# An attention-and-maxout kernel: stores moved between half-size DMA transposes, loads one batch earlier, a warmed-up head

## The chip, the cores and the metric

The kernel runs on one core of a Trainium2 chip. A core has five engines that run their own instruction streams and wait for each other through semaphores: TensorE (PE, matrix products), VectorE (DVE), ScalarE (ACT), GpSimd (POOL) and SyncE (SP), which only issues transfers. Sixteen DMA engines move data between the main memory (HBM), and the on-chip memory (SBUF), and inside SBUF. Matrix products land in PSUM, eight banks of 128 x 512 float32, and VectorE or ScalarE must copy them out ("evict") before a bank can be used again.

A transfer is started by an engine's instruction stream. GpSimd builds its descriptors in software ("software queue" below), SyncE in hardware ("hardware queue"). A stream is in order: an instruction that waits holds up all that stand behind it on that engine, transfers included.

The metric is device time in microseconds, the median of several runs.

## The reference

Four batches of 12544 rows of 128 numbers. First an induced-set attention: 32 learned points attend to all rows (`h`), then all rows attend to these 32 results. Then a maxout layer on each row.

```python
h = mab(I, x)                 # softmax(I x^T / sqrt(128)) x : 32 x 128 for each batch
y = mab(x, h)                 # softmax(x h^T / sqrt(128)) h : 12544 x 128 for each batch
# maxout on all 50176 rows, d_ff = 1024
h1 = y @ w1
h2 = y @ w2
g = np.maximum(h1, h2)
out = g @ w_out
```

Since `y = a h / sum(a)`, with `a` the 32 exponentials of a row, and the sum is positive, the kernel never forms `y`. It uses max(h1, h2) = h1 + relu(h2 - h1), so

    out = (a (h w1 w_out) + relu(a (h (w2 - w1))) w_out) / sum(a)

The first term needs only a 32 x 128 matrix for each batch (called m1 in the code, from w1*w_out); the second needs a product of depth 32, a relu of 1024 numbers for each row, and a product of depth 1024.

## The kernel before

A batch is 98 chunks of 128 rows. Phase 1 of a batch (the sums that give h) must be complete before its second part can begin; so phase 1 of batch b+1 is put between the work of batch b. The program is ordered by hand: a small model of the engines' times in the Python code (`ck`) decides in which order the instructions are issued; the chip sees only that order and the waits.

Loads convert float32 to float16 on the way, in 14-chunk parts (7 for each batch), into 12 buffers `xn`. The scores need x transposed (`xT`, two tiles, one for even and one for odd batches). In batch 0 TensorE transposes; for batches 1 to 3 a DMA transpose does.

```python
    outp = ctx.enter_context(tc.tile_pool(name="outp", bufs=5))     # output tiles, 128 x 512 f32
    ...
    def load_x(b, i):
        k0, n = parts[b][i]
        nc.gpsimd.dma_start(out=xn_at[b, i][:, 0:n, :], in_=xr[b, :, k0 : k0 + n, :])

    def transpose_x_dma(b, i):
        k0, n = parts[b][i]
        nc.sync.dma_start_transpose(xT_tiles[b % 2][:, k0 : k0 + n, :], xn_at[b, i][:, 0:n, :])
```

The head. TensorE transposes batch 0 (`p1_transpose`, L216; VectorE copies the first half of each part out of PSUM, L220, ScalarE the second, L223), makes the scores (L232), ScalarE takes the exponential (L241), and two accumulations in PSUM sum up (L253, L262). Then the weights:

```python
        n0 = len(parts[0])                      # 8 parts in batch 0
        for i in range(n0):
            p1_transpose(0, i)
            if i > 0:
                p1_accum(0, i - 1)
            p1_scores(0, i)
        p1_accum(0, n0 - 1)
        for i in range(7):
            load_x(1, i)
        small_h(0)                              # h of batch 0
        weights_1()                             # w2 - w1
        small_hwd(0)                            # hwd = h (w2 - w1), L336
        ...
        for i in range(7):
            transpose_x_dma(1, i)
        stage(blocks[0])                        # exponentials a of a block of rows, L449 and L461
        weights_2()                             # w1 transposed, L376; copies on ScalarE, L369 and L380
        weights_3()                             # w1*w_out, L387
        small_m1(0)                             # m1 = h w1 w_out, L350; m1bd, L357
        nstage = 1
```

The main loop. A block is four quarters of rows (four groups of 32 rows of the TensorE array work at once). `phase` (L718) makes four relu inputs of 128 x 512, in four PSUM banks; ScalarE (L734) or VectorE (L737), whichever the model has free earlier, evicts each with a relu: one such eviction is a "unit", worth four of the 128 x 128 products that follow. `final_one` (L562) multiplies with w_out, eight products for each chunk of 128 rows; a group of four chunks is then scaled by 1/sum(a) on VectorE into an output tile and stored:

```python
        def evict_group(g, end):
            osb = outp.tile([128, 4, C], F32, name=f"o_{uid[0]}", tag="o")
            nc.vector.tensor_mul(osb[...], g.ps[...], rp)                    # L588 and two more forms
            ...
            for b, c, s, m in runs:
                eng = nc.sync if b == B - 1 else nc.gpsimd
                eng.dma_start(out=outr[b, :, c : c + m, :], in_=osb[:, s : s + m, :])   # L614
            chunks_done[0] += n
```

The side work is called by the number of chunks done:

```python
        for b in range(1, B):
            base = DONE0[b - 1]                          # 0, 98, 196
            step, first = (5, 14) if b == 1 else (7, 4)
            for i in range(7):
                at(base + first + step * i, p1_scores, b, i)          # reads xT, part i
                at(base + first + step * i + 2, p1_accum, b, i)       # reads xn, part i
            end = base + first + step * 6
            at(end + 3, small_fold, b)                   # GpSimd: folds the sums of exponentials, L293, L294
            at(end + 5, small_h, b)                      # TensorE, L313: reads the fold
            at(end + 6, small_hwd, b)
            at(end + 7, small_m1, b)
            if b + 1 < B:
                for i in range(7):
                    at(base + 20 + 6 * i, load_x, b + 1, i)

        def staged_all(b):                               # when the last block of batch b is staged
            if 0 <= b and b + 2 < B:
                for i in range(7):
                    transpose_x_dma(b + 2, i)            # xT tile of batch b is free again
```

Between the accumulations, GpSimd adds up the exponentials of phase 1 (L283, L288). In this kernel all stores of batches 0 to 2 and all loads are GpSimd's; SyncE has the transposes and the stores of batch 3.

Of the kernel before, what the change touches and what calls it, by code (L numbers as in the profile page):

```python
# [9 lines left out]
F16 = mybir.dt.float16  # L10
# [98 lines left out]
def kernel(  # L109
# [15 lines left out]
    assert C == 128 and M == 32 and NJB == 8 and N % 128 == 0 and K == 98 and B == 4  # L125
    scale = 1.0 / math.sqrt(C)
    P1 = 14

    consts = ctx.enter_context(tc.tile_pool(name="consts", bufs=1))
    big = ctx.enter_context(tc.tile_pool(name="big", bufs=1))  # L130
# [1 line left out]
    e2p = ctx.enter_context(tc.tile_pool(name="e2p", bufs=4))  # L132
    smp = ctx.enter_context(tc.tile_pool(name="smp", bufs=2))
    relup = ctx.enter_context(tc.tile_pool(name="relup", bufs=2))
    outp = ctx.enter_context(tc.tile_pool(name="outp", bufs=5))
    rpp = ctx.enter_context(tc.tile_pool(name="rpp", bufs=4))
    psum = ctx.enter_context(tc.tile_pool(name="psum", bufs=1, space=bass.MemoryType.PSUM))

# [6 lines left out]
    def bank(shape, dtype=F32, only=None):  # L145
        i = min(range(8), key=lambda j: ck.bank[j]) if only is None else only
        uid[0] += 1
        return i, psum.tile(shape, dtype, name=f"ps{uid[0]}", tag=f"bank{i}", bufs=1)
# [14 lines left out]
        k0, n = parts[b][i]  # L163
        nc.gpsimd.dma_start(out=xn_at[b, i][:, 0:n, :], in_=xr[b, :, k0 : k0 + n, :])  # L164

    def transpose_x_dma(b, i):
        k0, n = parts[b][i]
        nc.sync.dma_start_transpose(xT_tiles[b % 2][:, k0 : k0 + n, :], xn_at[b, i][:, 0:n, :])

    identity16 = consts.tile([128, 128], F16, name="identity16")  # L170
    identity32 = consts.tile([128, 128], F32, name="identity32")
    ones32 = consts.tile([128, 128], F32, name="ones32")
    ones16 = consts.tile([128, 128], F16, name="ones16")
    ones_q = consts.tile([128, 4], F16, name="ones_q")

    ind_sb = consts.tile([M, C], F32, name="ind_sb")
# [11 lines left out]
    with tc.manual_schedule(engines={ET.PE, ET.DVE, ET.Activation, ET.Pool, ET.SP}):  # L188
# [7 lines left out]
        nc.gpsimd.dma_start(out=w2f, in_=moe_w2)  # L196
        nc.gpsimd.dma_start(out=w1f, in_=moe_w1)
        nc.gpsimd.dma_start(out=woutf, in_=moe_w_out.rearrange("(jb j) c -> j jb c", j=128))
        nc.vector.memset(ones16, 1.0)
        nc.vector.memset(ones32, 1.0)  # L200
        nc.vector.memset(ones_q, 0.0)
# [7 lines left out]
        def p1_transpose(b, i):  # L209
            k0, n = parts[b][i]  # L210
            xn = xn_at[b, i]
            h = (n + 1) // 2
            for g, m in ((0, h), (h, n - h)):
                bi, ps = bank([128, 8, 128], F16)
                for j in range(m):
                    nc.tensor.transpose(ps[:, j, :], xn[:, g + j, :], identity16)  # L216
                end = ck.run(0.056 * m, ready=ck.bank[bi], why="T")
                dst = xT_tiles[b % 2][:, k0 + g : k0 + g + m, :]
                if g == 0:
                    nc.vector.tensor_copy(out=dst, in_=ps[:, 0:m, :])  # L220
                    ck.bank[bi] = ck.on_dve(end, 0.08 + 0.075 * m)
                else:
                    nc.scalar.copy(out=dst, in_=ps[:, 0:m, :])  # L223
                    ck.bank[bi] = ck.on_act(end, 0.05 + 0.12 * m)
                st[b]["xT", i] = max(ck.bank[bi], st[b].get(("xT", i), 0.0))
# [170 lines left out]
            ck.bank[bi] = ck.on_dve(end, 0.2)  # L396


        bi, ps = bank([128, 512])
        nc.tensor.transpose(ps[:, 0:M], ind_sb, identity32[0:M, 0:M])  # L400
        nc.vector.tensor_copy(out=inducingT, in_=ps[:, 0:M])
        ck.bank[bi] = 0.0
        for n in ("h", "e"):
            st[0][n + "b"], st[0][n + "ps"] = bank([128, 512])
            ck.bank[st[0][n + "b"]] = INF
        n0 = len(parts[0])
        for i in range(n0):
            p1_transpose(0, i)
            if i > 0:
                p1_accum(0, i - 1)  # L410
            p1_scores(0, i)
        p1_accum(0, n0 - 1)
        for i in range(7):
            load_x(1, i)
        small_h(0)
        weights_1()
        small_hwd(0)


        blocks = []  # L420
        for b in range(B):
            c0 = 0
# [12 lines left out]
        def stage(blk):  # L435
            bi, ps = bank([128, 512])
            wd = blk.width
            some = [qu for qu in blk.quarters if qu]
            ck.wait(max(ck.bank[bi], st[some[0].b]["hT4r"]), "stage bank")
            for q in range(4):  # L440
                qu = blk.quarters[q] or some[0]
                hq = st[qu.b]["hT4"][:, 32 * q : 32 * (q + 1)]
                xT = xT_tiles[qu.b % 2]
                lo = qu.c0 if qu.c0 + wd <= K else K - wd
                pieces = [(0, qu.c0, min(wd, K - qu.c0))]
                if pieces[0][2] < wd:
                    pieces.append((pieces[0][2], lo, wd - pieces[0][2]))
                for t, c, n in pieces:
                    nc.tensor.matmul(  # L449
                        out=ps[32 * q : 32 * (q + 1), 128 * t : 128 * (t + n)],  # L450
                        lhsT=hq,
                        rhs=xT[:, c : c + n, :],
                        start=True,
                        stop=True,
                        tile_position=(0, 32 * q),
                        skip_group_check=True,
                    )
            end = ck.run(0.054 * wd, "col")
            uid[0] += 1
            blk.e2 = e2p.tile([128, 512], F16, name=f"e2_{uid[0]}", tag="e2")  # L460
            nc.scalar.activation(  # L461
                out=blk.e2[:, 0 : 128 * wd], in_=ps[:, 0 : 128 * wd], func=AF.Exp, scale=scale
            )
            blk.staged = ck.bank[bi] = ck.on_act(end, 0.05 + wd * 128 / 1200.0)
            blk.staged = max([blk.staged] + [st[qu.b]["hwdr"] for qu in some])
            blk.relu = {}

        relu_of = {}
# [1 line left out]
        def relu_slot(blk, q):  # L470

            if q in blk.relu:
                return blk.relu[q]
            w = blk.quarters[q].w
            tag = f"relu{q}" if w > 1 else f"rs{q}"
            past = relu_of.setdefault(tag, [])
            if len(past) >= 2 and past[-2].last_group[q] >= state["g"]:
                return None
            past.append(blk)
            uid[0] += 1  # L480
            blk.relu[q] = relup.tile([128, 1024 * (w if w == 1 else 4)], F16, name=f"relu_{uid[0]}", tag=tag)
            return blk.relu[q]

        def dens(blk):
            bi, ps = bank([128, 512])
            ck.wait(ck.bank[bi], "den bank")
            wd = blk.width
            for t in range(wd):
                nc.tensor.matmul(
                    out=ps[:, 4 * t : 4 * t + 4],  # L490
                    lhsT=blk.e2[:, 128 * t : 128 * (t + 1)],
                    rhs=ones_q,
                    start=True,
                    stop=True,
                )
            end = ck.run(0.029 * wd)
            uid[0] += 1
            blk.rp = rpp.tile([128, 4, 4], F32, name=f"rp_{uid[0]}", tag="rp")
            nc.vector.reciprocal(
                out=blk.rp[:, 0:wd, :].rearrange("p t q -> p (t q)"), in_=ps[:, 0 : 4 * wd]  # L500
            )
            ck.bank[bi] = ck.on_dve(end, 0.2)


        groups = [g for blk in blocks for g in blk.groups]
# [72 lines left out]
        def evict_group(g, end):  # L578
# [31 lines left out]
                else:  # L610
                    runs.append([qu.b, c, s, 1])
            for b, c, s, m in runs:
                eng = nc.sync if b == B - 1 else nc.gpsimd
                eng.dma_start(out=outr[b, :, c : c + m, :], in_=osb[:, s : s + m, :])  # L614
            chunks_done[0] += n

        def finals_left():
# [131 lines left out]

        for b in range(1, B):  # L750
            base = DONE0[b - 1]
            step, first = (5, 14) if b == 1 else (7, 4)
            for i in range(7):
                at(base + first + step * i, p1_scores, b, i)
                at(base + first + step * i + 2, p1_accum, b, i)
            end = base + first + step * 6
            at(end + 3, small_fold, b)
            at(end + 5, small_h, b)
            at(end + 6, small_hwd, b)
            at(end + 7, small_m1, b)  # L760
            if b + 1 < B:
                for i in range(7):
                    at(base + 20 + 6 * i, load_x, b + 1, i)

        def staged_all(b):
            if 0 <= b and b + 2 < B:
                for i in range(7):
                    transpose_x_dma(b + 2, i)

        pending = []  # L770

# [15 lines left out]
                pending.pop(0)  # L787
                f(*a)

        for i in range(7):  # L790
            transpose_x_dma(1, i)
        stage(blocks[0])
        weights_2()
        weights_3()
        small_m1(0)
        nstage = 1
        START = ck.pe
        while state["g"] < len(groups):
            side_work()
            need = [ptr[q][0] for q in range(4)]  # L800
            if nstage < len(blocks):
# [6 lines left out]
                if min(left) <= 3 and free and min(ck.bank) <= ck.pe + 0.1 and all(  # L808
                    "hT4" in st[qu.b] and "hwd" in st[qu.b] for qu in blocks[nstage].quarters if qu
                ):  # L810
                    stage(blocks[nstage])
                    nstage += 1
                    if nstage < len(blocks) and blocks[nstage].b != blocks[nstage - 1].b:
                        staged_all(blocks[nstage - 1].b)
                    continue
            jobs = plan_phase()
            tp = INF
# [48 lines left out]
```

## Time and profile before

| what | value |
|---|---|
| median of 3 runs | 386.44 us (375.67, 386.44, 393.12) |
| profiled run | 381.42 us, span of the core 379.6 us |
| TensorE busy | 344.5 us, 91% of the span |
| VectorE, ScalarE busy | 287.7 us (76%), 280.1 us (74%) |
| GpSimd busy | 84.2 us (22%) |
| DMA, software queue | 33.69 MB, 38.3% of 16 engines |
| DMA, hardware queue | 16.08 MB, 31.8% of 16 engines |
| transposes (21), us from issue to landing | median 9.3 |
| stores from GpSimd (72 of 256 KB), the same | median 4.5 |
| stores from SyncE (24 of 256 KB), the same | median 2.0 |

How to read it: "busy" of TensorE is modelled, since its products are pipelined, and is not a measure of how near it is to its peak. The profile's page cuts the span into 40 slices of 9.5 us; each digit is a tenth of the slice:

```profile
PE   2968999998979999996974899999699999999996
DVE  1244899997845999993852699889589989999982
ACT  2647899986945989973771489888489888899860
DMA  7999999999999324999999992212112222222223
```

Three stretches are seen: the head (slices 1 to 4), a long middle in which the DMA engines are busy nearly all of the time with one pause, and an end in which they are not. Lines such as L614 are those of the kernel before.

### The profile page before, as it was taken

The numbers are of one execution on the slowest core, as the hardware profiler recorded it, in microseconds if no ns is written. First come the engines' busy times: TensorE is split into PE (matmuls) and PEld (weight loads), VectorE is DVE, ScalarE is ACT, GpSimd is POOL, SyncE is SP. The second block draws the span as 40 slices with busy tenths as digits, with TensorE's granted clock in tenths as the row PEclk, the third lists the DMA queues.
The fourth block names the chain that finished last, engine by engine and source line by source line (L and its number), as shares of the span: only waits on it lengthen the run. The fifth ranks groups of instructions, "written<-read, shape, count | busy, mean of one in ns | idle before, by whom it ended". The sixth has DMA issues, their size and how long they took to land.

```text
span 379.6 us, 12988 instructions
## 1 busy us (share of the span) xinstructions
PE 344.5 (91%) x5643; PEld 266.5 (70%) x5643; DVE 287.7 (76%) x523; ACT 280.1 (74%) x546; POOL 84.2 (22%) x144
## 2 busy tenths in 40 slices
PE   2968999998979999996974899999699999999996
PEld 2856776776766777775753677778577777777786
DVE  1244899997845999993852699889589989999982
ACT  2647899986945989973771489888489888899860
POOL 6320122543111124552110112323311120000000
PEclk9996999999998999996996699999999999999999
DMA  7999999999999324999999992212112222222223
GB/s 139 219 281 204 213 213 190 191 198 181 128 125 157 127 85 90 190 217 102 118 124 79 142 188 96 85 70 102 58 57 85 86 98 112 86 85 86 96 102 126
DMA packets 52521, 50.60 MB, mean 133 GB/s; under 512 B 40432, under 2 KB 40720, under 8 KB 52464
## 3 DMA queue, kind: packets, MB, share of 16 engines
q0 software_dynamic: 10512, 33.69, 38.3%
q1 hardware_dynamic: 41952, 16.08, 31.8%
q8 instruction: 44, 0.72, 0.8%
q14 instruction: 13, 0.11, 0.1%
HBM read 27.28 MB, written 25.69 MB: 140 GB/s over the span
## 4 chain that ended last, share of the span: by engine, by line
PE 67%; DMA 13%; issue 9%; ACT 5%; POOL 3%; DVE 2%; POOLq 0%; ACTq 0%; DVEq 0%
PE ps L562 41%; PE ps L718 16%; DMA out_dram<-o 11%; ACT relu L734 2%; PE ps L232 2%; PE ps L216 2%; PE ps L449 2%; PE ps L275 2%; ACT xT L223 1%; DMA xn<-in_x_dram 1%; POOL out_dram L614 1%; PE ps L550 1%; POOL xn L164 1%; DVE o L588 1%; ACT et L241 1%
## 5 line engine op out<-in xcount | busy, mean ns | idle before, releaser
L734 ACT ACTIVATE relu<-ps 128x512 f16<-128x512 f32 x454 | 241.6, 603 | 64.5 <-PE ps L718 59.6
L737 DVE TENSOR_SCALAR relu<-ps 128x512 f16<-128x512 f32 x330 | 213.0, 682 | 25.6 <-PE ps L718 23.8
L562 PE MATMUL ps<-woutp,relu 128*128 128x128 f16 x3136 | 231.4, 224 | 0.3 <-ACT relu L734 0.3
L562 PEld LDWEIGHTS <-relu 128*128 128x128 f16 x3136 | 184.9, 100 | 41.6 <-issue 31.7
L718 PE MATMUL ps<-e,hwd 32*128 32x512 f16 (+2 forms) x928 | 95.7, 357 | 11.2 <-DVE o L588 9.9
L614 POOL DMA_DIRECT2D out_dram<-o x75 | 40.8, 545 | 214.2 <-DVE o L588 103.4
L588 DVE TENSOR_TENSOR o<-ps,rp 128x512 f32<-128x512 f32 x88 | 60.1, 684 | 28.2 <-DMA out_dram<-o 20.8
L718 PEld LDWEIGHTS <-hwd 32*128 32x128 f16 x928 | 26.5, 92 | 26.3 <-issue 7.3
L718 PE MATMUL ps<-m,e 32*128 32x128 f16 x336 | 33.8, 219 | 1.3 <-DVE o L588 1.3
L718 PEld LDWEIGHTS <-e 32*128 32x128 f16 x336 | 19.0, 93 | 12.4 <-issue 10.1
L241 ACT ACTIVATE et<-ps 128x448 f16<-128x448 f32 (+2 forms) x29 | 15.7, 541 | 5.8 <-PE ps L232 5.5
L288 POOL TENSOR_TENSOR eacc<-eacc,et 128x448 f32<-128x448 f32 x18 | 18.9, 1048 | 0.3
L164 POOL DMA_DIRECT2D xn<-in_x_dram x29 | 15.9, 554 | 7.7 <-DMA xn<-in_x_dram 4.5
L232 PE MATMUL ps<-inducingT,xT 128*128 128x32 f16 x392 | 15.4, 178 | 1.6 <-ACT xT L223 1.6
L461 ACT ACTIVATE e<-ps 128x512 f16<-128x512 f32 (+2 forms) x31 | 16.5, 533 | 0.0
L220 DVE COPY xT<-ps 128x896 f16<-128x896 f16 (+2 forms) x8 | 4.5, 566 | 14.9 <-PE ps L216 14.9
L232 PEld LDWEIGHTS <-xT 128*128 128x128 f16 x392 | 13.2, 97 | 2.5 <-ACT xT L223 2.2
L223 ACT COPY xT<-ps 128x896 f16<-128x896 f16 (+2 forms) x8 | 6.5, 811 | 8.6 <-PE ps L216 8.6
L449 PE MATMUL ps<-xT,hT 128*32 128x512 f16 (+2 forms) x124 | 11.2, 350 | 0.0
L216 PE MATMUL ps<-identity,xn 128*128 128x128 f16 x98 | 8.9, 258 | 2.4 <-DMA xn<-in_x_dram 2.4
L313 PE MATMUL ps<-eacc,ones 128*128 128x32 f32 x24 | 4.1, 323 | 7.6 <-POOL eacc L294 7.6
L275 PE MATMUL ps<-et,xn 128*128 128x32 f16 x294 | 10.6, 176 | 0.0
(59 smaller groups left out, 115.5 us busy)
## 6 DMA issues: line engine op xcount, KB each, us to landing
out_dram<-o POOLq DMA_DIRECT2D x72, 256.0 KB, 4.5
xn<-in_x_dram POOLq DMA_DIRECT2D x27, 448.0 KB, 9.0
out_dram<-o SPq DMA_DIRECT2D x24, 256.0 KB, 2.0
wf<-in_moe_w_dram POOLq DMA_DIRECT2D x2, 512.0 KB, 14.0
wof<-in_moe_w_out_dram POOLq DMA_DIRECT2D x1, 512.0 KB, 12.9
out_dram<-o POOLq DMA_DIRECT2D x3, 128.0 KB, 2.1
xT<-xn SPq DMA_TRANSPOSE x21, 9.3
xn<-in_x_dram POOLq DMA_DIRECT2D x1, 256.0 KB, 13.3
```

The lines of the kernel that those rows point to most:

```text
L164: nc.gpsimd.dma_start(out=xn_at[b, i][:, 0:n, :], in_=xr[b, :, k0 : k0 + n, :])
L232: nc.tensor.matmul(out=ps[:, j * M : (j + 1) * M], lhsT=xT_tiles[b % 2][:, k0 + j, :], rhs=inducingT, start=True, stop=True,)
L241: nc.scalar.activation(out=et[:, 0:n, :], in_=ps[:, 0 : n * M], func=AF.Exp, scale=scale)
L275: nc.tensor.matmul(out=ps[:, 0:M], lhsT=xn[:, j, :], rhs=et[:, j, :], start=(j == 0), stop=(j == n - 1))
L288: nc.gpsimd.tensor_add(out=acc, in0=acc, in1=et)
L449: nc.tensor.matmul(out=ps[32 * q : 32 * (q + 1), 128 * t : 128 * (t + n)], lhsT=hq, rhs=xT[:, c : c + n, :], start=True, stop=True, tile_p ...
L562: nc.tensor.matmul(out=g.ps[:, 128 * c : 128 * (c + 1)], lhsT=g.blk.relu[q][:, 128 * (jb * w4 + t) : 128 * (jb * w4 + t + 1)], rhs=woutp[: ...
L588: nc.vector.tensor_mul(osb[:, 0:n, :], g.ps[:, 0 : n * C].rearrange("p (s c) -> p s c", s=n), rp)
L614: eng.dma_start(out=outr[b, :, c : c + m, :], in_=osb[:, s : s + m, :])
L718: nc.tensor.matmul(**seq[i])
L734: nc.scalar.activation(out=dst, in_=src, func=AF.Relu)
L737: nc.vector.tensor_scalar(out=dst, in0=src, scalar1=0.0, scalar2=None, op0=ALU.max)
```

## The change

Five things are changed together.

- Stores all go through SyncE. The transposes, also SyncE's, are cut into halves (7 chunks each), and called one by one by the number of chunks done, so that in SyncE's stream a half transpose stands behind a store and a store behind a half transpose. What is meant: no store has to share the DMA engines with a long row of transposes, and GpSimd's stream is free for loads and sums. There are six output tiles instead of five.
- Loads of batch b are called from 26 chunks before the end of batch b-2 (batch 2: from chunk 72 of the whole on), every six chunks, and transposes from 16 chunks before that end, every four chunks; for batch 1 from chunk 1 on, every three. Phase 1 is spread a little otherwise.
- At the head, 12 products on a tile of zeros are put before the first real one, to have TensorE awake.
- After `hwd`, two phases of the first block are issued before the weights of the first term (w1*w_out) are made; the first block is staged before w2 - w1.
- VectorE copies 8 of 14 transposed chunks in the head and ScalarE 6, instead of 7 and 7; relu tiles of narrow blocks are shared differently, which makes room for the sixth output tile and the zeros.

```diff
+    WARM = 12
...
-    outp = ctx.enter_context(tc.tile_pool(name="outp", bufs=5))
+    outp = ctx.enter_context(tc.tile_pool(name="outp", bufs=6))
...
-    def transpose_x_dma(b, i):
+    def transpose_x_dma(b, j):
+        i, h = divmod(j, 2)
         k0, n = parts[b][i]
-        nc.sync.dma_start_transpose(xT_tiles[b % 2][:, k0 : k0 + n, :], xn_at[b, i][:, 0:n, :])
+        m = n // 2
+        nc.sync.dma_start_transpose(
+            xT_tiles[b % 2][:, k0 + m * h : k0 + m * (h + 1), :], xn_at[b, i][:, m * h : m * (h + 1), :]
+        )
...
-            h = (n + 1) // 2
+            h = min(8, (n + 2) // 2)
...
-            tag = f"relu{q}" if w > 1 else f"rs{q}"
+            small = w == 1 and blk.index >= 4
+            tag, bufs = (f"rs{q % 2}", 1) if small else (f"relu{q}", 2)
...
+        bi, ps = bank([128, 512])
+        for _ in range(WARM):
+            nc.tensor.matmul(out=ps, lhsT=warm[:, 0:128], rhs=warm, start=True, stop=True)
...                                              # the head, moved behind the definitions
         small_h(0)
+        stage(blocks[0])
         weights_1()
         small_hwd(0)
...
-                eng = nc.sync if b == B - 1 else nc.gpsimd
-                eng.dma_start(out=outr[b, :, c : c + m, :], in_=osb[:, s : s + m, :])
+                nc.sync.dma_start(out=outr[b, :, c : c + m, :], in_=osb[:, s : s + m, :])
...
-            step, first = (5, 14) if b == 1 else (7, 4)
+            p_first, p_step = (10, 6.3) if b == 1 else (2, 7)
+            t_first, t_step = (1, 3) if b == 1 else (-16, 4)
             for i in range(7):
-                at(base + first + step * i, p1_scores, b, i)
-                at(base + first + step * i + 2, p1_accum, b, i)
+                s = int(p_first + p_step * i)
+                at(base + s, p1_scores, b, i)
+                at(base + s + 2, p1_accum, b, i)
...
-            if b + 1 < B:
+            for j in range(14):
+                at(base + t_first + t_step * j, transpose_x_dma, b, j)
+            if b > 1:
                 for i in range(7):
-                    at(base + 20 + 6 * i, load_x, b + 1, i)
-
-        def staged_all(b):
-            if 0 <= b and b + 2 < B:
-                for i in range(7):
-                    transpose_x_dma(b + 2, i)
+                    at(base - 26 + 6 * i, load_x, b, i)
...
-        for i in range(7):
-            transpose_x_dma(1, i)
-        stage(blocks[0])
+        phase(plan_phase())
+        phase(plan_phase())
+        stage(blocks[1])
         weights_2()
         weights_3()
         small_m1(0)
-        nstage = 1
+        nstage = 2
```

Where a store and the transposes called after it meet in SyncE's stream of the changed kernel: at the start of batch 0 one or two half transposes between two stores, and for batches 2 and 3 mostly one, each behind a store of four chunks.

## The prediction

> **What bounds the kernel now.** I read the windows of ten microseconds first, because the average hides that the stages differ. The columns are busy time of each engine with its number of instructions, then granted clock, DMA share (1.00 is 16 busy engines) and GB/s.
>
> ```profile
> 130.00:140.00 10.00, 10.00 (x176) 7.45 (x176) 9.38 (x17) 9.28 (x20) 1.64 (x3) 1.00 0.15 56
> ...
> 170.00:180.00 10.00, 6.71 (x67) 5.11 (x65) 4.32 (x10) 3.73 (x8) 2.97 (x5) 0.73 1.27 105
> 180.00:190.00 10.00, 9.92 (x145) 7.29 (x143) 8.18 (x15) 7.90 (x19) 1.84 (x4) 0.93 1.30 120
> 190.00:200.00 10.00, 6.74 (x105) 4.74 (x100) 4.72 (x8) 7.39 (x16) 0.86 (x2) 0.92 1.18 124
> 200.00:210.00 10.00, 4.67 (x44) 3.68 (x44) 2.98 (x5) 1.57 (x3) 0.54 (x1) 0.67 1.23 83
> ```
>
> At 130 us TensorE, VectorE and ScalarE are all above 90% and the DMA engines nearly idle: the compute bound. From 170 to 210 us every compute engine starves while the DMA engines are over-full and move only 83 to 124 GB/s. So second I read the chain of waits there (start, length, what):
>
> ```profile
> 175.81 0.56 POOL xn L164
> 176.36 7.27 issue
> 183.65 25.76 DMA out_dram<-o
> 209.46 0.04 issue
> ```
>
> One store of 256 KB takes 25.76 us; with five output buffers, VectorE can't evict the next group until it lands. Third I asked how long issues took to land, by stretch. For 164 to 213 us the transposes' line (min/median/max), then the stores' line:
>
> ```profile
> DMA to landing us min/median/max: 10.2/25.0/39.9
> ...
> DMA to landing us min/median/max: 5.8/20.9/26.4
> ```
>
> and the stores from 230 to 311 us, with no transpose in flight:
>
> ```profile
> DMA to landing us min/median/max: 2.3/2.3/4.4
> ```
>
> A store is nine times slower beside transposes in this stretch. All seven transposes of a batch are put in SyncE's queue at once, when the batch two earlier has been staged, while GpSimd issues stores and loads on the software queue. In the trace's packets, a 256-byte transpose packet takes 24 to 27 ns at 40 to 60 us and 73 to 201 ns on average at 170 to 210 us: mixing two backlogged queues makes the DMA engines inefficient, it doesn't merely share them. A milder episode lies at 92 to 121 us (store latency median 16.8 us).
>
> Last, the waits between 268 and 281 us, the point where a batch's sums are folded:
>
> ```profile
> ACT relu L734 <- PE ps L718: 5.3, 2, 4.9
> ...
> PE ps L313 <- POOL eacc L294: 3.1, 1, 3.1
> ```
>
> GpSimd's fold stands behind a store in its in-order queue, and TensorE waits for it.
>
> **What the Trainium skill says.** "DMA: Bandwidth & Descriptors", section "Queues, rings and completion order": each DMA engine takes the queues that have work in turn, packet by packet, while in one ring descriptors are consumed in order. The trace agrees that software and hardware queues interleave; the page doesn't predict the collapse to 83 GB/s. The same page, section "SWDGE vs HWDGE vs iDMA": a DMA that casts must come from GpSimd, so the float32-to-float16 loads stay there and only stores move. "TensorE: Matmul & The Clock Gate", section "What's actually happening": the array runs at half clock until it has been busy for some 3.4 us. In the chain of waits the first three groups of 14 input transposes take 1.69, 1.51 and 1.51 us and later ones 0.81 us: agrees. The same section has it drop back after an idle window; the granted clock of 0.67 at 200 us agrees.
>
> **The change part by part.** I build the new time from stretches of the kernel before that ran undisturbed, using the issue times of the stores in the trace (each stands for four chunks of 128 rows) as a clock.
>
> 1. *Head, idle matmuls.* 12 matmuls on zeros run from about 1.5 us (my estimate: VectorE's first memset could start at 0.8 us), while TensorE otherwise waits for the first load (landed at 6.31 us), so they cost nothing. With a warm clock each part needs 2.13 us (15.09 to 17.22 in the chain) instead of 2.9, so the last part follows the loads: the sixth lands at 17.93, plus 2.13 and 1.6 for the last two parts gives 21.7 instead of 22.92. Gain 1.2 us. Giving VectorE eight of 14 and ScalarE six makes ScalarE's 0.91 us copy about 0.8; included as nothing.
>
> 2. *Head, order.* Before, the relu work begins at 32.5 us because weights (transposes of w1, copies, the product w1*w_out) stand first. After, two phases (eight relu units) go before them, from about 27.4 us. The first final group still needs w1*w_out, through ScalarE's copies (1.05 and 1.13 us) now behind five relus (2.7 us), so it isn't earlier: about 35 instead of 34.5. But eight units are ready, worth 2.6 us of the two relu engines, of which I count 1.5 us. Against it I put 1 us for the relu buffers: the first two blocks now take theirs from the same pair as the next blocks, so the next must wait for them. First store: 40.65 - 1.2 - 1.5 + 1 = 39 us.
>
> 3. *Batch 0.* Its first 48 chunks, with the sums of batch 1 beside them, took from 40.65 to 86.67, 46 us. Spread more thinly (every 6.3 chunks instead of 5): 45. Then the fold gap, estimated 5 us: before, 8.5 us (stores at 270.95 and 279.49) of which the fold wait is 3.1; with no stores in GpSimd's queue it should shrink. Then the second half at the rate of 279.49 to 310.02, 30.5 us. Ends at 119.5 instead of 128.
>
> 4. *Batches 1 and 2.* The model is batch 2 before, which ran with the transposes already done: 3 us over the boundary, 40.3 us for 48 chunks with sums, 5.5 us gap, 30.5 us: 79.3 us each, against 99.7 (127.99 to 227.65) and 82.4 us. That gives 278.
>
> 5. *Batch 3 and tail.* Nothing changes: 3.2 us over the boundary, then 313.2 to 376.9, then 2.7 us to the end of the span. 278 + 3.2 + 63.7 + 2.7 = 347.7.
>
> So the span falls by 32 us: 20.4 of batch 1, 8.5 - 1.65 = 6.9 of batch 0, 3.1 of batch 2, 1.65 of the head. The device time is about 1.8 us above the span (381.42 to 379.6): 349.5.
>
> Costs: 21 whole transposes become 42 halves; SyncE took 1.8 to 3.75 us to put out a whole one, and 100 stores at 0.33 to 0.37 us are 35 us more on a queue that was otherwise waiting. None is on the chain unless SyncE blocks.
>
> **The rivals.**
> *A, the change as intended:* stores and transposes share one ring in order, at most one or two half transposes are put between stores, and the queue can't backlog because every transpose stands behind a store that waits for output. 350 us.
> *B, the collapse stays in small:* loads are still on the software queue. Alone, loads land 2.15 us apart (6.31 to 19.95, eight), half a transpose is about 1.35 us of all engines (896 packets of 24 ns over 16), a store 0.68. At 0.67 us a chunk, with a load every six chunks and a half transpose and a store every four, that asks for 54 + 50 + 25 = 129% of the DMA engines for the 16 chunks between the first transpose and the batch's end, and about 104% for ten more. Six output buffers cover some 16 us, the backlog is 3 to 5 us if packets stay efficient. If they go to 70 to 200 ns again, one stall per batch returns, 8 to 10 us each in batches 0 and 1: 365 to 370.
> *C, the new head-of-line wait:* a store stands behind a transpose that waits for its load or for old readers of its tile, or the sums of batch b run into an xT part not yet transposed. The last part has its second half issued at chunk 134 and is read at 142, some 6 us later, and 1.5 to 4 us would do. For it speaks that everything now hangs in one queue; against it that the loads are called ten chunks ahead and the old tile's readers are long done. 358 to 375.
> *D, the stalls were hidden:* the lag of up to 38 units between relu and final products could have made up for them. Against it: 29 final products in 200 to 210 us against 97 to 101 at 230 to 260 us, and nothing afterwards runs faster than usual. Then 375.
>
> **Range and chances.** A has about two thirds, B a fifth, C and D the rest. Weighted: 0.66 x 349 + 0.2 x 367 + 0.1 x 366 + 0.04 x 375 = 355, but B in its weakest form is likeliest, so the middle is 351, with 339 to 365 for 8 in 10. Before has a median of 386.44 and runs from 375.67 to 393.12; 2% below is 378.7, above nearly all rivals. Faster 0.94, same 0.04, slower 0.02.
>
> **What would show each step.** In the windows, no ten microseconds between 45 and 360 us with TensorE under 85% busy except at the three folds; stores landing within 6 us in every stretch; no wait of VectorE on the output DMA (before: 20.8 us); the fold wait of TensorE under 3 us in all (before: 7.6); the input transposes at 0.8 us per 14 from the first part; the first store at 38 to 40 us. Wrong it is if transposes again take over 10 us to land, if VectorE waits for stores in batches 0 and 1 (B), if SyncE's waits show a transpose that stores queue behind (C), or if batches 1 and 2 take over 85 us though DMA is calm (a compute bound I misread).

## The result, and the profile after

| | before | changed |
|---|---|---|
| median | 382.51 us (4 runs, 375.67 to 393.12) | 359.56 us (4 runs, 358.61 to 362.34) |
| ratio | | 0.954, 95% interval 0.945 to 0.963 |
| profiled run | 381.42 us, span 379.6 | 362.34 us, span 360.6 |

The change brings 4.6% (3.7 to 5.5). Predicted were 351 us, with 339 to 365 as range. Some executions of a kernel take over 1.5% longer than its fastest one; ratios leave these out, medians do not. In the windows of the changed kernel (engines as before: PE, PEld, DVE, ACT, POOL, then granted clock, DMA share, GB/s) the long starved stretch of before has no counterpart at 170 to 210 us; the starved stretches are shorter and lie elsewhere.

```profile
130.00:140.00 10.00, 6.62 (x125) 5.22 (x123) 6.35 (x11) 6.36 (x13) 1.03 (x1) 1.00 1.11 123
140.00:150.00 10.00, 8.60 (x109) 6.33 (x110) 5.70 (x11) 5.33 (x11) 1.03 (x1) 0.66 0.63 172
...
190.00:200.00 10.00, 10.00 (x176) 7.97 (x173) 9.25 (x17) 8.89 (x19) 0.00 (x0) 1.00 0.29 108
200.00:210.00 10.00, 10.00 (x166) 7.82 (x164) 9.35 (x17) 8.88 (x18) 0.00 (x0) 1.00 0.73 143
210.00:220.00 10.00, 10.00 (x183) 7.52 (x180) 9.41 (x18) 9.15 (x19) 1.62 (x3) 1.00 1.12 164
220.00:230.00 10.00, 8.31 (x140) 6.60 (x138) 6.30 (x12) 6.38 (x13) 2.06 (x2) 0.83 1.18 191
```

The chain of waits of the changed kernel at 124 to 146 us names the holder (start, length, what):

```profile
126.64 0.62 PE ps L575 x11
128.47 12.88 DMA xT<-xn
141.77 0.55 PE ps L730 x4
```

It is a half transpose now, not a store. The waits agree: VectorE no longer waits for output tiles (20.8 us before), and TensorE waits for xT instead, a wait that the kernel before does not have:

```profile
PE ps L239 <- DMA xT<-xn: 8.1, 4, 4.8
```

What holds that transpose up is seen in GpSimd's timeline (start, length, instruction, and in brackets how long the engine was idle and for whom):

```profile
85.78 0.39 POOL L301 TENSOR_TENSOR eacc<-eacc 128x96 f32<-128x96 f32 x1
86.26 2.69 POOL L165 DMA_DIRECT2D xn<-in_x_dram  x5
127.52 0.56 POOL L290 CAST eacc<-et 128x448 f32<-128x448 f16 x1 [38.57 <-ACT et L248]
128.09 0.54 POOL L165 DMA_DIRECT2D xn<-in_x_dram  x1
129.03 0.53 POOL L165 DMA_DIRECT2D xn<-in_x_dram  x1 [0.41 <-PE ps L730]
```

Five of batch 2's seven loads are issued together at 86 us, right after the fold of batch 1 (the thirteenth store, at 87.77 us, stands for 48 chunks done, not 72), and two wait some 40 us more, because in GpSimd's stream they stand behind the cast L290, which needs the first exponentials of batch 2. They are then issued into the middle of the half transposes. (So the loads are not called "one batch earlier", as the title has it: batch 2's are called from chunk 72 on, before from chunk 20 on.) The same happens at 214 us for batch 3. Counting by "chunks done" fixes an order in each stream; it is not a time. For stores and transposes, order behind a store does pace; a load on GpSimd has nothing in front of it that waits for output any more.

### The profile page after: what moved, and what is told of

It reads as the page before. It is cut to its first block, busy times and chain, and to the rows that moved or that the text cites. A ratio compares the mean times of both kernels' runs of the same rounds, so it can differ in the third digit from the quotient of the medians.

```text
span 360.6 us, 13062 instructions
## 1 busy us (share of the span) xinstructions
PE 339.7 (94%) x5655; PEld 260.9 (72%) x5655; DVE 291.1 (81%) x529; ACT 277.1 (77%) x541; POOL 43.2 (12%) x69
## 4 chain that ended last, share of the span: by engine, by line
PE 78%; DMA 12%; ACT 4%; DVE 3%; issue 1%; POOL 1%; SPq 1%; POOLq 0%; ACTq 0%; DVEq 0%
PE ps L575 50%; PE ps L730 18%; DMA xT<-xn 9%; DMA xn<-in_x_dram 3%; PE ps L435 2%; ACT relu L746 2%; PE ps L239 2%; PE ps L282 2%; DVE relu L749 2%; PE ps L563 1%; PE ps L476 1%; PE ps L320 1%; PE ps L223 0%; ACT xT L230 0%; POOL xn L165 0%
## 5 line engine op out<-in xcount | busy, mean ns | idle before, releaser
L746 ACT ACTIVATE relu<-ps 128x512 f16<-128x512 f32 x449 | 238.5, 601 | 42.0 <-PE ps L730 37.0
L749 DVE TENSOR_SCALAR relu<-ps 128x512 f16<-128x512 f32 x335 | 215.6, 682 | 32.9 <-PE ps L730 28.8
L575 PE MATMUL ps<-woutp,relu 128*128 128x128 f16 x3136 | 226.9, 222 | 0.1
L575 PEld LDWEIGHTS <-relu 128*128 128x128 f16 x3136 | 181.0, 99 | 39.5 <-issue 29.7
L730 PE MATMUL ps<-e,hwd 32*128 32x512 f16 (+2 forms) x928 | 91.6, 359 | 0.4 <-DVE hwd L346 0.4
L227 DVE COPY xT<-ps 128x1024 f16<-128x1024 f16 (+2 forms) x8 | 5.1, 633 | 11.7 <-PE ps L223 11.7
L290 POOL CAST eacc<-et 128x448 f32<-128x448 f16 x3 | 1.7, 558 | 101.0 <-ACT et L248 101.0
L230 ACT COPY xT<-ps 128x768 f16<-128x768 f16 (+2 forms) x8 | 5.6, 705 | 8.5 <-PE ps L223 8.5
L282 PEld LDWEIGHTS <-xn 128*128 128x128 f16 x294 | 9.9, 97 | 0.1
L223 PE MATMUL ps<-identity,xn 128*128 128x128 f16 x98 | 6.8, 219 | 1.9 <-DMA xn<-in_x_dram 1.9
```

The lines of the kernel that those rows point to most:

```text
L282: nc.tensor.matmul(out=ps[:, 0:M], lhsT=xn[:, j, :], rhs=et[:, j, :], start=(j == 0), stop=(j == n - 1))
L575: nc.tensor.matmul(out=g.ps[:, 128 * c : 128 * (c + 1)], lhsT=g.blk.relu[q][:, 128 * (jb * w4 + t) : 128 * (jb * w4 + t + 1)], rhs=woutp[: ...
L730: nc.tensor.matmul(**seq[i])
L746: nc.scalar.activation(out=dst, in_=src, func=AF.Relu)
L749: nc.vector.tensor_scalar(out=dst, in0=src, scalar1=0.0, scalar2=None, op0=ALU.max)
```

## The experiments

Theory: what SyncE issues starves while GpSimd's software queue has a backlog, so it matters from which queue the stores come and when the loads do, and two late loads for each batch account for most of the missing gain. Rivals: the pacing or the halving did it; the shared ring has waits of its own; the head's parts count for more. Edits are against the changed kernel unless said otherwise.

### Loads called earlier

```diff
-                    at(base - 26 + 6 * i, load_x, b, i)
+                    at(base - 26 + 4 * i, load_x, b, i)
```

> The changed kernel with one number altered: loads of batches 2 and 3 called every 4 chunks instead of every 6, so that in GpSimd's stream all seven stand ahead of the cast (L290) that begins the sums of their batch. Theory 1 (two late loads collide with half transposes): the transposes issued at 128 and 214 us, which took 12.9 and 10.9 us to land, land within 5 us, TensorE's wait on xT (8.1 us in all) falls to about 3 us, which is batch 1's alone, and the time falls from 359.6 to 348 to 352 us. Theory 2 (transposes and stores in one ring hold each other up, loads don't matter): the same waits remain, time within 1.5 us of 359.6. Theory 3 (seven loads in a row now delay the stores): stores at 86 to 105 us take over 12 us, VectorE waits for output tiles, time 360 or more.

Measured: 352.8 us (352.36 to 356.27), ratio 0.933 (0.919 to 0.947), just above the range of theory 1. To rule out the chip, it was run again beside the changed kernel:

> The changed kernel as it is, for comparison on the chip of these runs: 357 to 362 us here, or up to 370 if the chip's transfers are as slow as where the whole transposes took 370 us.

> The changed kernel with loads called every 4 chunks instead of 6, beside the changed kernel on one chip. If the two late loads of each of batches 2 and 3 are what kept the change from its predicted time: 6 to 8 us under the changed kernel of this call. If the earlier 352.8 us was the chip's: less than 3 us.

Measured on one chip, six runs each: changed kernel 359.06 us, ratio 0.949 (0.940 to 0.957); early loads 352.73 us, ratio 0.934 (0.929 to 0.939): 6.3 us of difference, or 6.0 without the changed kernel's longest run (361.12). In GpSimd's timeline of the early loads, all seven precede the cast:

```profile
87.46 3.23 POOL L165 DMA_DIRECT2D xn<-in_x_dram  x6
90.94 0.54 POOL L165 DMA_DIRECT2D xn<-in_x_dram  x1 [0.25 <-issue]
128.74 0.56 POOL L290 CAST eacc<-et 128x448 f32<-128x448 f16 x1 [37.26 <-ACT et L248]
```

and the windows of 130 to 150 us are full:

```profile
130.00:140.00 10.00, 10.00 (x185) 7.65 (x180) 8.98 (x18) 9.21 (x18) 2.07 (x2) 1.00 0.89 173
140.00:150.00 10.00, 10.00 (x185) 7.62 (x183) 9.33 (x18) 8.98 (x18) 1.03 (x1) 1.00 0.64 115
```

TensorE's wait on xT is 1.7 us instead of 8.1, and no transpose of batches 2 and 3 takes over 4.7 us: none of them is in flight together with a load. Theory 1 holds; theory 3's price was not paid (stores beside the seven loads land within 9.2 us, which six output tiles cover).

### Stores back on GpSimd

```diff
-                nc.sync.dma_start(out=outr[b, :, c : c + m, :], in_=osb[:, s : s + m, :])
+                eng = nc.sync if b == B - 1 else nc.gpsimd
+                eng.dma_start(out=outr[b, :, c : c + m, :], in_=osb[:, s : s + m, :])
```

> The changed kernel with the stores of batches 0 to 2 back on GpSimd; half transposes, their pacing, six output tiles and the head as changed. Theory 1 (the store's own queue matters: a software queue with a backlog starves what SyncE issues, as transposes beside 7 loads took 12 to 20 us in the bare transfers): transposes beside stores and loads take over 8 us again, TensorE waits for xT more than the 8.1 us of the changed kernel, 366 to 374 us. Theory 2 (pacing alone brought the gain, no backlog builds up when a transpose stands behind a number of finished chunks): within 3 us of 359.6. Here the loads stand between stores in GpSimd's stream and so are paced by output, which may help.

Measured: 405.51 us (389.35 to 408.94), before on the same chip 394.88 (382.2 to 402.27); the fastest executions are 389.35 and 382.2, too few comparable ones for an interval. With the stores back on GpSimd nothing of the gain is left. But the edit alters more than a queue. With no store in SyncE's stream nothing there waits for output, so the pacing goes too: the transposes of batch 1 are issued from 26.8 us on, in the changed kernel from 41.1. And the loads of batch 2, now behind stores in GpSimd's stream, are issued one by one from 110 to 147 us, where the changed kernel issues five together at 86. The waits of the profiled run (404.06 us), then the transposes' time to land (min/median/max) from 110 to 160 us, beside these loads, and from 165.3 to 180 us, when the loads have landed and GpSimd still stores:

```profile
PE ps L239 <- DMA xT<-xn: 32.8, 10, 11.0
...
DMA to landing us min/median/max: 8.0/19.6/29.8
...
DMA to landing us min/median/max: 3.9/4.6/5.7
```

Beside loads and stores of the software queue a half transpose takes six times as long as alone (19.6 us against 3.1, stage B below), beside GpSimd's stores without loads one and a half times (4.6), and the sums of the next batch run into the late ones. Theory 1 is right in kind, its 366 to 374 us are far exceeded; theory 2 is not tested, since the pacing is gone.

### The kernel before, with its stores on SyncE

```diff
-                eng = nc.sync if b == B - 1 else nc.gpsimd      # kernel before
+                eng = nc.sync
```

> The kernel before with one line altered: all stores on SyncE, transposes whole and put out seven at once as before. Theory 1 (order in the one queue matters): stores stand behind transposes that wait for their loads, which GpSimd now issues without pause, so blocks of some 20 us: 375 to 400 us, VectorE waiting for output tiles over 20 us. Theory 2 (it was the mixing of stores and transposes in two queues alone): 362 to 368 us.

Measured: 369.96 us (368.12 to 370.62), ratio 0.966 (0.959 to 0.972). Neither theory's number: one line gives most of the gain. The wait I expected is there but small: the first store is issued at 56.67 us instead of 40.65, behind the seven transposes of batch 1, which SyncE has put out by 56.56 us, and VectorE waits 14.0 us for output tiles. From 164 to 213 us, where before a store took 20.9 us in the median and a transpose 25.0, transposes and stores take:

```profile
DMA to landing us min/median/max: 4.2/5.6/6.1
...
DMA to landing us min/median/max: 2.0/3.7/6.0
```

This is not the old traffic in another queue, though. No store holds up GpSimd any more, so the last two of batch 3's seven loads are issued at 179.4 us, and each of the seven lands within 7.2 us:

```profile
179.39 1.10 POOL L164 DMA_DIRECT2D xn<-in_x_dram  x2
...
DMA to landing us min/median/max: 4.7/6.8/7.2
```

The transposes, now behind stores, come after them, from 193.9 us on; in the kernel before loads were in flight beside transposes until 211.75 us. Counted over whole profiles, by the times of issue and landing:

| kernel | transposes in flight with a load, their median us | without a load |
|---|---|---|
| before (whole transposes) | 14, 11.1 | 7, 7.0 |
| before, stores on SyncE (whole) | 4, 8.1 | 17, 5.6 |
| changed, stores back on GpSimd (halves) | 19, 13.8 | 23, 4.5 |
| changed (halves) | 7, 10.9 | 35, 3.7 |
| changed, early loads (halves) | 0 | 42, 3.3 |

In each kernel that has both, the transposes beside loads are the slow ones, and the stores' move decides how many meet a load. Without a load, those beside GpSimd's stores take 7.0 and 4.5 us and those that share SyncE's queue with the stores 5.6 and 3.7, a smaller difference.

### Whole transposes

```diff
-    def transpose_x_dma(b, j):
+    def transpose_x_dma(b, i):
...                                                     # and its body as in the kernel before
-            for j in range(14):
-                at(base + t_first + t_step * j, transpose_x_dma, b, j)
+            for i in range(7):
+                at(base + t_first + t_step * (2 * i + 1), transpose_x_dma, b, i)   # 14 chunks at once
```

> The changed kernel with whole transposes, each called where the second half of its part was called; stores on SyncE as changed. If halves matter because a store waits behind at most one of them: stores behind a whole transpose land about 1.3 us later (half of the 2.6 us that a whole one holds the queue), which six output tiles hide; 359 to 362 us, with longer waits of the first sums of batch 1 on xT. If the size matters for the engines as such: over 366 us.

Measured: 370.21 us (367.27 to 372.84), ratio 0.962 (0.949 to 0.975), on the chip on which the stores' move alone gave 0.966: with whole transposes and two late loads for each batch, pacing, the sixth output tile and the new head together show no gain over that move. The interval overlaps with the changed kernel's, so on halves it settles nothing; with early loads, beside early loads and halves on one chip:

> Early loads with whole transposes. If halves matter through the sums that wait for their part of xT (13.7 us of TensorE's waits with whole ones and late loads, 8.1 us with halves): 5 to 9 us over the kernel with early loads and halves. If they only mattered beside the late loads: within 2 us.

Measured: 355.42 us (352.83 to 357.12) against 352.73 (352.02 to 353.77): halves are worth about 2.7 us, and most of it lies in batch 0's first 48 chunks (50.0 us from first to thirteenth store against 47.6). TensorE's waits for xT, 2.8 us against 1.7, are less than half of it; the rest was not traced. The difference lies between the two expectations.

### The head

```diff
-    WARM = 12
+    WARM = 0
```

> The changed kernel without the 12 products on zeros. My step: the first groups of 14 input transposes take 1.5 us again and the last part of batch 0 begins 1.2 us later, so 360.5 to 361 us. Rival: the loads pace the head whatever the clock, difference under 0.5 us.

Measured: 359.29 us (356.49 to 362.04), ratio 0.947 (0.909 to 0.984). No difference can be seen. The clock did follow: the first 14 input transposes take 0.95 us with the idle products and 1.67 without, but the fifth group, which waits 1.31 us for its load, starts only 0.7 us earlier (16.41 us instead of 17.11), the sixth likewise (18.42 instead of 19.11), and at the first store 0.14 us are left (40.71 and 40.85).

```diff
-        phase(plan_phase())
-        phase(plan_phase())
-        stage(blocks[1])
         weights_2()
         weights_3()
         small_m1(0)
+        phase(plan_phase())
+        phase(plan_phase())
+        stage(blocks[1])
```

> The changed kernel with the two early phases put back behind the weights of the first term (w1*w_out); all else as changed. If the early phases bring what I counted (1.5 us): 361 us. If they only push ScalarE's weight copies behind five relus and leave TensorE idle and at half clock (first final product at 36.2 us against 34.5 us before): 358 us or less, and the first store at about 39 us instead of 40.7.

> Early loads, and the two early phases put back behind the weights. In the traces the first final product comes at 36.0 us with early phases and at 35.1 us without, although the sums of batch 0 ended 1.8 us later in that run. If the early phases cost: 1 to 2.5 us under the kernel with early loads alone. If the eight units made ahead pay, as I predicted (1.5 us): 1 to 2 us over it.

Measured: 357.83 us (354.97 to 367.29), ratio 0.941 (0.923 to 0.959), by itself; with early loads 352.10 (350.14 to 353.22) against 352.73. The two cannot be told apart. With early phases first (timeline, early loads) the first final products come at

```profile
36.37 2.12 PE L575 MATMUL ps<-woutp,relu 128*128 128x128 f16 x18
```

and with the weights first at

```profile
34.24 0.31 PE L575 MATMUL ps<-woutp,relu 128*128 128x128 f16 x1
```

so 2.1 us earlier, but little comes of it: the first store is at 40.82 us with weights first and 41.40 with phases first, the thirteenth at 89.22 and 88.98.

### Transfers alone

Two kernels hold only transfers of the same sizes, stage after stage, each begun when the one before has landed; they compute nothing and leave the output unfilled.

> Transfers alone, nothing computed, output not filled: seven stages, each begun when the one before has landed. A: 7 loads with conversion from GpSimd. B: 14 half transposes from SyncE. C: A and B at once. D: 14 half transposes with 10 stores from GpSimd. E: 14 half transposes with 10 stores, alternating, all from SyncE. F: E with 7 loads beside. G: 10 stores from SyncE. Theory 1 (mixing transposes with a backlogged software queue makes the engines inefficient): A 15 us, B about 20, C longer than A + B (over 36 us), D over B + 7, E about B + 7 = 27, F over 45. Theory 2 (they only share): C about 35 at most and packets of 256 bytes keep their 24 ns when queueing is left out; D and E alike, F about A + B + 7 = 42.

> Transfers alone, output not filled. H: 7 whole transposes. I: H beside 7 loads. J: H beside 10 stores from GpSimd. K: H beside 10 stores and 7 loads, alternating, from GpSimd. L: K with 14 half transposes. With halves the bare transfers only took turns: 35.8 us for transposes and loads against 38.2 one after the other, and 29.0 for transposes and stores against 28.6. If whole transposes or the three together make the engines inefficient, as the kernel before at 170 to 210 us with 83 to 124 GB/s: K well over H + 17.8 + 8.2, that is over 50 us, under 130 GB/s. If they only take turns: K and L 40 to 46 us, over 180 GB/s, and the inefficiency of the kernel before comes from something else, such as the compute engines' own traffic.

| stage | us from first issue to last landing |
|---|---|
| A 7 loads / B 14 halves / G 10 stores from SyncE / H 7 whole | 17.8 / 20.4 / 8.2 / 17.2 |
| C loads and halves (A + B = 38.2) | 35.8 |
| D halves, stores from GpSimd (B + G = 28.6) | 29.0 |
| E halves and stores, both from SyncE | 26.3 |
| F as E, with loads (A + B + G = 46.4) | 41.7 |
| I whole and loads (35.0) / J whole and stores of GpSimd (25.4) | 33.5 / 27.6 |
| K whole, stores and loads of GpSimd (43.2) | 41.9 |
| L halves, the same (46.4) | 49.8 |

(G stands for the stores of GpSimd in the sums too.) The sums are nearly kept: the engines mostly take turns and lose little. What differs is who waits. Time to land of the half transposes in the first kernel that were issued while the stage's other transfers ran, in the stages B, C, D and E (14, 4, 6 and 14 of them):

```profile
DMA to landing us min/median/max: 2.9/3.1/3.2
...
DMA to landing us min/median/max: 12.5/15.1/19.8
...
DMA to landing us min/median/max: 3.4/6.1/13.5
...
DMA to landing us min/median/max: 2.9/3.0/3.2
```

Beside a store of its own queue a transpose takes what it takes alone; beside a backlog of loads on the software queue five times that, beside one of stores twice. The packets show it: alone, transposes put through 612 packets of 256 bytes a microsecond; in C, while the loads last, 101, beside 43 load packets of 3584 bytes (50 alone); in D 234, beside 39 store packets of 4096 bytes. So the queue with small packets gets its turns but not its bytes: 26 of 182 GB/s in C. The Trainium skill says that each DMA engine goes round the queues that have work, a packet at a time ("DMA: Bandwidth & Descriptors", section "Queues, rings and completion order"); that neither queue stops agrees with it, but it gives no ratio like the 2.3 and 6.0 small packets for each large one here. In F, a store behind such a transpose in SyncE's queue takes up to 18.4 us. Theory 2 of the first kernel holds for the sums of C and F, nearly, though D and E are not alike; neither foresaw the starving. In the second kernel K is within the 40 to 46 us of mere turns, and L is not.

## Why the prediction was right or wrong

The middle was 351 us, the changed kernel takes 359.6. That is inside the range, but not because rival A came true: of the signs that the prediction named, transposes took over 10 us to land again (up to 12.9), a store took 10.9 us, not at most 6, and TensorE was only 66% busy from 130 to 140 us. By the issue times of the stores in the profiled run, which is 2.8 us above the median (span 360.57, predicted 347.7), the 12.9 us of difference are:

- *Head* (step 1 and 2): first store at 40.71 us, predicted 39: +1.7. Both gains were mis-sized. The idle products were to bring 1.2 us and brought 0.7 at the sixth group and nothing that can be measured at the end. The early phases were to bring 1.5 us and bring nothing that can be told (beside early loads 352.73 us with them, 352.10 without): ScalarE's five relus push the weight copies back, as the step itself said. TensorE's granted clock at 30 to 40 us is low either way, 0.57 in the changed kernel and 0.59 with early loads and the weights first.
- *Batch 0* (step 3): first 48 chunks 47.07 us, predicted 45; second half with fold 35.40, predicted 35.5: +2.0. Phase 1's thinner spread bought nothing, and sums waited for half transposes at 48 and 68 us. The 35.40 is right by luck: the fold gap is 2.98 us instead of 5, the rest 32.4 instead of 30.5.
- *Batch 1* (step 4): 88.0 us from the last store of batch 0 to its own last, predicted 79.3: +8.7. Its first 48 chunks took 47.50 instead of 40.3 us, and 40.12 with early loads. This is the step that failed: it took over a stretch of the kernel before in which no transpose ran, and, as said under C, trusted that "the loads are called ten chunks ahead"; a load called then is not a load issued then. With batch 2's share it is worth the 6 us between the kernels of one chip.
- *Batch 2*: 79.5, predicted 79.3, but by a compensation: 43.45 instead of 40.3 for its first 48 chunks (late loads again; 40.26 with early ones), less at the fold and the boundary.
- *Batch 3 and tail* (step 5): 69.9, predicted 69.6.

That the stores' move ends the starved stretch was right, and so was where the gain lies (batches 0 and 1). Two parts of the reasoning behind it do not stand. First, "mixing two backlogged queues makes the DMA engines inefficient, it doesn't merely share them": the bare transfers mix them too, and show turns at nearly full use and a starved queue. So mixing alone does not explain how slow the kernel before was from 170 to 210 us: 21 packets a microsecond of the software queue beside 99 of transposes, against 50 and 131 in stage K. The changed kernel has such a stretch too, 123 GB/s at 130 to 140 us against 194 in stage F. Where that remainder comes from (the compute engines' use of the memory is one candidate) was not tried. Second, the pacing: rival A said that the queue can't backlog because each transpose stands behind a store. It backlogged at 128 us all the same, behind two loads; and on one chip the time is 370 us with the stores on SyncE and no pacing, and 370 with pacing and whole transposes.

So most of the gain comes from the stores' move, shown by one line, and the missing part from the late loads, shown by one number. How the move acts stays open between two things that it brings at once: stores and transposes share a queue, and loads and transposes come to lie apart in time. The table of transposes with and without a load speaks for the second as the larger. A kernel with its stores on GpSimd and its loads kept away from the transposes would settle it and was not run. Halves are a refinement of about 3 us.

Rival B (a stall left by the loads on the software queue) had a fifth; it is what happened, in batches 1 and 2 rather than 0 and 1. (Its 2.15 us between loads do not follow from "6.31 to 19.95, eight", which gives 1.95; in stage A, alone, loads landed 2.15 us apart.) C's head-of-line wait exists (a store behind a starved transpose took 10.9 us at 131 us), but as a consequence of B: with early loads it is gone. D is out: the time is 15 us under its 375.

The best kernels here are those with early loads: 352.7 us, or 352.1 with the weights first too, ratios 0.934 (0.929 to 0.939) and 0.932 (0.926 to 0.938).

## What to carry to other kernels

In these runs a transfer of small packets on one queue starved beside a backlog of large packets on another, while the total hardly suffered. So issue bulk loads where no DMA transpose is in flight (half transposes beside loads took 10.9 us in the median, with early loads 3.3), and prefer to put stores in the transposes' queue (3.0 us in stage E, 6.1 beside GpSimd's stores in D). A place in an in-order stream is not a time: look at what stands before a load in the stream of the engine that issues it. Before crediting pacing or tile sizes, move the one line that changes the queue and see how much is left; then look at what else that line has moved in time.

## What the runs showed that was not expected

Half transposes use the engines worse than whole ones beside a mixed backlog of the software queue: stage L took 49.8 us and K 41.9 for the same bytes, with 187 GB/s against 223 while the backlog lasted; alone the two differ less (20.4 us for 14 halves and 17.2 us for 7 whole). Each stage ran once. And beside loads, transposes got 72 (F) to 131 (K) packets a microsecond in the bare stages and 99 in the kernel before from 170 to 210 us, that is, by an estimate from these rates, 7 to 12 us for a half one (896 packets); beside GpSimd's stores without loads they got 234 (D) and 255 (J).
